# Five unsplit weight pairs, a reciprocal on ScalarE, the attention state kept in the keys' rows, port waits both ways, and a new instruction order, in a fused attention and MLP kernel

## The chip, the cores and the metric

The kernel runs on one core of one Trainium2 chip. The metric is the time of one execution on the device in microseconds (us). Engines are named as the profile names them: PE (TensorE, the matmuls), PEld (its weight loads), DVE (VectorE), ACT (ScalarE), POOL (GpSimd), SP (SyncE, which here only issues DMAs). Each engine carries out its own instruction list in order, and waits on semaphores for the others.

## The reference

Two stages. The first is a gated linear attention with a recurrence over 768 steps; the second is an MLP with a rational activation on the result.

```python
# q, k, v, alpha: (4, 8, 768, 48)
for t in range(S):
    state = alpha[:, :, t, :, None] * state + np.einsum('bhd,bhe->bhde', k[:, :, t], v[:, :, t])
    y[:, :, t] = np.einsum('bhd,bhde->bhe', q[:, :, t], state)
x = y.transpose(0, 2, 1, 3).reshape(3072, 384)
h = x @ w_in                       # w_in (384, 2048)
P = a[0] + a[1] * h + a[2] * h**2 + a[3] * h**3
Q = 1.0 + abs(b[0]) * abs(h) + abs(b[1]) * h**2
out = (P / (Q + 1e-06)) @ w_out    # w_out (2048, 384)
```

## The kernel before

**Attention.** The 3072 tokens are handled in 24 chunks of 128 tokens (g = 0 to 23, six for each batch entry). For a chunk, DVE forms running products of alpha with two scans (`suf`, line 470, and `pre`, line 482), which POOL or DVE multiply into k and q (`k`, line 491, and `q`, line 494). PE transposes k (`kt`), forms scores within each half chunk (`s`), the k-v products of both halves (`vk`) and at last the output (`am`, line 594). The state between chunks goes through three steps: `d` (line 564, POOL) multiplies the old state `st_s` by the chunk's total decay and writes it into the rows of the tile `sv` that `am` reads for the first half; `km` (line 605, DVE) adds the first half's k-v product and writes the rows for the second half; `kv` (line 609, DVE) adds the second half's product and writes `st_s`. The heads stand in two row groups (j = 0 and 1), so each of the three steps is two instructions of 48 rows by 192 columns, and a small copy `tot` (line 553 on ACT, 555 on DVE) brings the totals of one row group into the other's rows first. After `am`, ACT and DVE bring the result from PSUM into the MLP's input as a rounded part and a remainder (`xh`, `xl`).

**MLP.** It consists of 96 units, u = 0 to 95; each yields 128x512 activations. In a "wide" unit (128 features by 512 tokens) products are formed in three passes on operands of type fp32r: both operands are split into a rounded part and a remainder, and input and output take nine matmuls of 512 columns each (`in`, line 703; `oh` and `ol`, line 722, and lines 716 and 731 for the last 512 tokens). A "plain" unit (256 features by 256 tokens) uses unsplit words: six matmuls of 256 columns on the way in (line 676), six on the way out (line 689), each with two PE records in the trace. `JP = 4` pairs of feature blocks are worked plain for the first two token groups, which makes units 0 to 7 plain; unit 8 is the first wide one. Between `in` and `oh` a unit goes through ACT: `ah` (line 758), `t1` (761), `q1` (767, or POOL, 765); POOL: `qm` (770, the denominator); DVE: `t2` (781), `t3` (785); ACT: `ars` (788, one over the root), `sq` (791, its square, so an approximate reciprocal); DVE: `p` (795), `t` (798) and `g` (804), which correct the reciprocal and finish the quotient. Wide units need two steps more, the rounded part `gh` (807, ACT) and the remainder `gl` (811, POOL or DVE). The products `in` of unit u use a PSUM bank that `g` of unit u - 3 sets free.

**Weights.** Each pair of feature blocks has an input block (i0 to i7) and an output block (o0 to o7). They arrive as 64-bit words; ACT (`abs`, line 278), DVE (`low` 286, `sign` 292, or ACT 290, and `join` 306) make 32-bit words of them, and ACT and POOL split these (`hi` 321, `lo` 326). A plain pair's words are kept, and brought back later by a DMA to be split for the wide units.

**Order.** All of it is about 2,800 steps. A table of numbers (`ORDER`) gives the order in which `Plan.run` writes them out, and a bit for each says on which of two engines it runs. Some DVE steps are marked `lock` (the joins and shifts of the weights, the splits, and k, q and remainders where DVE does them): `Plan.run` makes the next POOL step in the table wait for such a step, and names as the reason a port that DVE and POOL share. A guard on alpha's range (`gu`, line 857, 36 ACT instructions), whose sum becomes the word `ok` (line 873), decides at the end whether a slow general path must run; it does not run here.

## Time and profile before

| | |
|---|---|
| median of 3 runs | 529.93 us (528.15 to 530.42) |
| profiled execution, whole | 529.12 us |
| its span, first to last instruction | 527.2 us |
| PE busy | 501.1 us, 95% |
| DVE busy | 492.3 us, 93% |
| ACT busy | 440.8 us, 84% |
| POOL busy | 424.8 us, 81% |
| mean granted PE clock | 0.993 |

Busy times are unions over the span. PE's matmuls overlap in their pipeline and their ends are modelled, so a stretch in which PE is busy throughout says that work follows work, not that it runs at its peak; the time from one matmul to the next is read from the chain, where matmuls in a row are merged into one piece with their count. The profiled execution took 1.92 us more than its span.

### The profile page before, as it was taken

The page shows a single profiled execution, that of the slowest core. Times are in us where ns is not written, and L with a number is a line of the kernel's source. Part 1 is how long each engine was busy: PE and PEld are TensorE (multiplying, and loading weights), DVE is VectorE, ACT ScalarE, POOL GpSimd, SP SyncE. Part 2 cuts the span into 40 slices and gives each one's busy share as a digit, 9 for nine tenths or more (in the row PEclk, how much of TensorE's full clock was granted, in tenths as well). Part 3 has the DMA queues.
Part 4 walks back from the last instruction along what each step waited for, and adds up shares of the span by engine and source line. Part 5 has one row for each costly group of instructions (what it writes and reads, how often), then busy time and mean ns, then how long its engine had stood idle before and what let it go on. Part 6 is the DMA issues. An engine that isn't in the chain of part 4 may idle for free.

```text
span 527.2 us, 13661 instructions
## 1 busy us (share of the span) xinstructions
PE 501.1 (95%) x5082; PEld 410.9 (78%) x5082; DVE 492.3 (93%) x773; ACT 440.8 (84%) x805; POOL 424.8 (81%) x421
## 2 busy tenths in 40 slices
PE   7877988988999999999999999999999999999996
PEld 7865876766878778787878778878888778888996
DVE  4999899999999999999999899999999999898885
ACT  4998999998999878887888798897888887987782
POOL 3556667899999998889879789888888887876782
PEclk9997999999999999999999999999999999999999
DMA  9989684565554444454446345351545201023001
GB/s 266 278 228 291 141 201 87 120 170 119 117 146 112 106 84 96 94 100 116 98 92 117 95 97 101 85 118 30 110 97 116 47 6 39 0 62 60 2 2 63
DMA packets 145656, 56.81 MB, mean 108 GB/s; under 512 B 133424, under 2 KB 138160, under 8 KB 145584
## 3 DMA queue, kind: packets, MB, share of 16 engines
q1 hardware_dynamic: 145440, 55.78, 45.1%
q8 instruction: 41, 0.67, 0.6%
...
HBM read 47.98 MB, written 4.72 MB: 100 GB/s over the span
## 4 chain that ended last, share of the span: by engine, by line
PE 76%; DVE 8%; DMA 5%; ACT 4%; SPq 3%; issue 2%; POOL 1%; DVEq 0%; POOLq 0%
PE ps L703 31%; PE ps L722 26%; PE ps L716 6%; PE ps L594 3%; DMA wi_words<-in_moe_w_in_dram 2%; PE ps L512 2%; SPq L409 2%; PE ps L689 2%; PE ps L576 2%; PE ps L545 1%; DMA raw_a<-in_alpha_dram 1%; ACT wo_words L290 1%; DVE t L804 1%; DMA wo_words<-in_moe_w_out_dram 1%; DVE ps L798 1%
## 5 line engine op out<-in xcount | busy, mean ns | idle before, releaser
L703 PE MATMUL ps<-x,wi 128*128 128x512 f32 x792 | 203.6, 397 | 2.8 <-DVE t L804 2.7
L703 PEld LDWEIGHTS ps<-x,wi 128*128 128x128 f32 x792 | 145.9, 188 | 36.2 <-DVE t L804 4.6
L722 PE MATMUL ps<-gh_gl,wo 128*128 128x512 f32 x648 | 170.1, 399 | 0.2 <-ACT gh_gl L807 0.2
L722 PEld LDWEIGHTS ps<-gh_gl,wo 128*128 128x128 f32 x648 | 119.2, 188 | 27.0 <-ACT gh_gl L807 0.3
L770 POOL TENSOR_TENSOR qm<-qm,ah 128x512 f32<-128x512 f32 x96 | 124.3, 1296 | 13.6 <-ACT qm L767 4.4
L811 POOL TENSOR_TENSOR gh_gl<-t,gh_gl 128x512 fp32r<-128x512 f32 x83 | 109.0, 1313 | 15.4 <-ACT gh_gl L807 12.7
L758 ACT ACTIVATE ah<-ps 128x512 f32<-128x512 f32 x96 | 57.2, 596 | 26.4 <-PE ps L703 25.8
L795 DVE SCALAR_TENSOR_TENSOR t<-t,coef,ps 128x512 f32<-128x512 f32 x96 | 70.6, 736 | 5.7 <-ACT ps L791 4.5
L761 ACT ACTIVATE t<-ps,coef 128x512 f32<-128x512 f32 x96 | 65.9, 687 | 8.5 <-PE ps L703 4.3
L785 DVE SCALAR_TENSOR_TENSOR t<-t,coef,ps 128x512 f32<-128x512 f32 x96 | 70.8, 739 | 1.0
L765 POOL TENSOR_SCALAR qm<-ah,bab 128x512 f32<-128x512 f32 x61 | 48.3, 793 | 29.0 <-ACT ah L758 15.8
L781 DVE TENSOR_TENSOR t<-t,ps 128x512 f32<-128x512 f32 x96 | 64.9, 676 | 4.6 <-ACT t L761 2.8
L788 ACT ACTIVATE ps<-qm 128x512 f32<-128x512 f32 x96 | 57.9, 604 | 12.6 <-DVE t L785 5.6
L804 DVE SCALAR_TENSOR_TENSOR t<-ps,t 128x512 f32<-128x512 f32 x96 | 65.5, 683 | 1.1
L798 DVE SCALAR_TENSOR_TENSOR ps<-qm,ps 128x512 f32<-128x512 f32 x96 | 65.8, 686 | 0.2
L807 ACT ACTIVATE gh_gl<-t 128x512 fp32r<-128x512 f32 x88 | 55.2, 628 | 5.8 <-DVE t L804 5.5
L791 ACT ACTIVATE ps<-ps 128x512 f32<-128x512 f32 x96 | 56.2, 586 | 2.0
L539 POOL TENSOR_SCALAR_AFFINE_SELECT tqk<-tqk 64x512 f32<-64x512 f32 x48 | 33.2, 692 | 12.7 <-ACT tqk L533 7.1
L470 DVE TENSOR_TENSOR_SCAN tg<-ta,ps 128x528 f32<-128x528 f32 x24 | 29.7, 1242 | 6.7 <-ACT ta L452 6.7
L494 POOL TENSOR_TENSOR tqk<-tqk,fp 128x512 f32<-128x512 f32 x22 | 29.1, 1322 | 7.2 <-DVE wi_words L306 6.1
L491 POOL TENSOR_TENSOR tqk<-tqk,tg 128x512 f32<-128x512 f32 x23 | 29.8, 1294 | 5.9 <-ACT tqk L452 5.5
L594 PEld LDWEIGHTS ps<-tqk,sv 128*32 128x32 f32 x1536 | 23.4, 112 | 13.8 <-issue 5.0
(112 smaller groups left out, 724.4 us busy)
## 6 DMA issues: line engine op xcount, KB each, us to landing
...
```

What stands on the lines that cost most here:

```text
L703: nc.tensor.matmul(h_of(u), w(key)[:, kt * FU + f % FU, :], x[:, kt, xp, :], start=(n == 0), stop=(n == len(todo) - 1),)
L722: nc.tensor.matmul(bank(O_BANKS[dt]), w(("o", f // FU))[:, f % FU, dt * P : (dt + 1) * P], g, start=(f == 0 and first_w), stop=(f == NF - ...
L758: nc.scalar.activation(buf(s, "ah", u), h_of(u), AF.Abs)
L761: nc.scalar.activation(buf(s, "t1", u), h_of(u), AF.Identity, bias=a2, scale=a3_reg)
L770: nc.gpsimd.tensor_tensor(buf(s, "qm", u), buf(s, "qm", u), buf(s, "ah", u), op=ALU.mult)
L781: nc.vector.tensor_tensor(t, t, h_of(u), op=ALU.mult)
L785: nc.vector.scalar_tensor_tensor(t, t, a1, h_of(u), op0=ALU.add, op1=ALU.mult)
L788: nc.scalar.activation(h_of(u), buf(s, "qm", u), AF.Abs_reciprocal_sqrt, bias=1.0 + 1e-6)
L795: nc.vector.scalar_tensor_tensor(t, t, a0, h_of(u), op0=ALU.add, op1=ALU.mult)
L798: nc.vector.scalar_tensor_tensor(h_of(u), buf(s, "qm", u), 1.0 + 1e-6, h_of(u), op0=ALU.add, op1=ALU.mult)
L804: nc.vector.scalar_tensor_tensor(t, h_of(u), 2.0, t, op0=ALU.subtract, op1=ALU.mult, reverse0=True)
L811: eng.tensor_tensor(buf(s, "gl", u).rearrange("p a b -> p (a b)"), buf(s, "t1", u), gh, op=ALU.subtract)
```

## The change

Five edits and a new table.

1. `JP = 5`: pairs 0 to 4 are plain for the first two token groups. Units 0 to 9 are plain, 10 to 95 wide.
2. `rcp` replaces `ars` and `sq`: one ACT instruction of the function Reciprocal. The coefficients are scaled by 2^-24 at the start, so that numerator and denominator stand at that scale.
3. The state stays in the rows in which the keys' products come (112 rows, both row groups and the gap between them): `d`, `km` and `kv` are one instruction each, of 112 rows by 192 columns, on three tiles `st`. New steps `dc` and `mc` (`place`) copy it into the rows of `sv`, two instructions of 48 rows by 192 columns each, on ACT or POOL: 50 instructions on ACT and 38 on POOL in the new table. `tot` and its tiles are gone.
4. `Plan.run` adds waits both ways: a locked step on DVE also waits for the last POOL step ahead of it in the table.
5. `one_eps`, `prime` and the waits are adapted to these.
6. `ORDER` is another table.

The diff, of the table only one line:

```diff
--- before.py
+++ after.py
@@ -51,3 +51,3 @@
         info = mybir.DependencyInfo(mybir.DependencyClass.Sync, mybir.DependencyReason.DATA)
-        held = None
+        held = last = None
         for n in order:
@@ -64,6 +64,11 @@
             if mode["lock"]:
+                if last is not None:
+                    tc.add_manual_dep(new[0], last.name, info, reason="shared port")
+                    last = None
                 held = new[-1]
-            elif mode["eng"] == "POOL" and held is not None:
-                tc.add_manual_dep(new[0], held.name, info, reason="shared port")
-                held = None
+            elif mode["eng"] == "POOL":
+                if held is not None:
+                    tc.add_manual_dep(new[0], held.name, info, reason="shared port")
+                    held = None
+                last = new[-1]
             done.add(key)
@@ -72,66 +77,64 @@
 ORDER = [
-    'c-jTQ1E3u`3;@t3X_~gPZQHhO+qS*k?fK2NZQHhO+xFi-XN*!Rx^gOtLN!)RQeLr&t;VUzDykZ<jGCubs3|I%TBxR~`D&t',
...
+    'c-jq?gO(*a5CGGi?sSs1ZQHhO+qS)XcV>35wr$(CZQHi--Zxa8Qx!=~R!X6YsiG-Sq*yr>Lm3rCMOS0hI5l3)SBunQ6;-WN',
...
 ]
@@ -166,3 +169,3 @@
 T2P = range(0)
-JP = 4
+JP = 5
 HALF = 3
@@ -232,4 +235,8 @@
 
+    SMALL = 2.0 ** -24
+    Q_ONE = (1.0 + 1e-6) * SMALL
+
     def abs_coef():
-        nc.scalar.activation(bab, coef[:, 4:6], AF.Abs)
+        nc.scalar.activation(coef[:, 0:4], coef[:, 0:4], AF.Copy, scale=SMALL)
+        nc.scalar.activation(bab, coef[:, 4:6], AF.Abs, scale=SMALL)
         load_reg(a3_reg, coef[0:1, 3:4])
@@ -357,5 +364,4 @@
     sv = ring("sv", NV, [P, 2, H, DP])
-    st_s = work.tile([P, H, D], F32, name="st_s")
-    tots = ring("tots", 2, [P, NC4])
     KW = P - GAP
+    st_0, st_m, st_e = ring("st", 3, [P, NC4, D])
     kts = ring("kt", NSC, [P, NC4 * KW + GAP])
@@ -549,17 +555,17 @@
 
-    def totals(eng, g):
-        o, x = tots[g % 2][rows_of(1)], totals_of(g)[rows_of(0)]
-        if eng is nc.scalar:
-            eng.activation(o, x, AF.Copy)
-        else:
-            eng.tensor_copy(o, x)
-
     def decay(eng, g):
-        o, r = state_of(g, 0), rows_of(1)
-        if first(g):
-            eng.memset(o, 0.0)
+        t = totals_of(g)[0:KW].unsqueeze(2).to_broadcast([KW, NC4, D])
+        eng.tensor_tensor(st_0[0:KW], st_e[0:KW], t, op=ALU.mult)
+
+    def place(eng, g, c):
+        o = state_of(g, c)
+        if c == 0 and first(g):
+            nc.gpsimd.memset(o, 0.0)
             return
         for j in range(2):
-            t = totals_of(g) if j else tots[g % 2]
-            eng.tensor_tensor(o[:, j::2], st_s[r, j::2], t[r].unsqueeze(2).to_broadcast([D, NC4, D]), op=ALU.mult)
+            x = (st_m if c else st_0)[rows_of(j)]
+            if eng is nc.scalar:
+                eng.activation(o[:, j::2], x, AF.Copy)
+            else:
+                eng.tensor_copy(o[:, j::2], x)
 
@@ -567,4 +573,4 @@
 
-    def kv_of(c, j):
-        return bank(SCB + c)[rows_of(j), KV0 : KV0 + NC4 * D].rearrange("p (a d) -> p a d", d=D)
+    def kv_of(c):
+        return bank(SCB + c)[0:KW, KV0 : KV0 + NC4 * D].rearrange("p (a d) -> p a d", d=D)
 
@@ -600,11 +606,9 @@
     def kv_mid(g):
-        for j in range(2):
-            if first(g):
-                nc.vector.tensor_copy(state_of(g, 1)[:, j::2], kv_of(0, j))
-            else:
-                nc.vector.tensor_tensor(state_of(g, 1)[:, j::2], state_of(g, 0)[:, j::2], kv_of(0, j), op=ALU.add)
+        if first(g):
+            nc.vector.tensor_copy(st_m[0:KW], kv_of(0))
+        else:
+            nc.vector.tensor_tensor(st_m[0:KW], st_0[0:KW], kv_of(0), op=ALU.add)
 
     def kv_add(g):
-        for j in range(2):
-            nc.vector.tensor_tensor(st_s[rows_of(1), j::2], state_of(g, 1)[:, j::2], kv_of(1, j), op=ALU.add)
+        nc.vector.tensor_tensor(st_e[0:KW], st_m[0:KW], kv_of(1), op=ALU.add)
 
@@ -786,7 +790,11 @@
 
-    def act_ars(u, s):
-        nc.scalar.activation(h_of(u), buf(s, "qm", u), AF.Abs_reciprocal_sqrt, bias=1.0 + 1e-6)
-
-    def act_sq(u, s):
-        nc.scalar.activation(h_of(u), h_of(u), AF.Square)
+    def inverse_of(o, x, bias):
+        imm = [mybir.ImmediateValue(dtype=F32, value=v) for v in (bias, 1.0, 0.0)]
+        nc.scalar.add_instruction(mybir.InstActivation(
+            name=nc.get_next_instruction_name(), engine=nc.scalar.engine, func=AF.Reciprocal,
+            ins=[nc.scalar.lower_ap(x), *imm], outs=[nc.scalar.lower_ap(o)],
+        ))
+
+    def act_rcp(u, s):
+        inverse_of(h_of(u), buf(s, "qm", u), Q_ONE)
 
@@ -798,3 +806,3 @@
         nc.vector.scalar_tensor_tensor(
-            h_of(u), buf(s, "qm", u), 1.0 + 1e-6, h_of(u), op0=ALU.add, op1=ALU.mult
+            h_of(u), buf(s, "qm", u), Q_ONE, h_of(u), op0=ALU.add, op1=ALU.mult
         )
@@ -949,3 +957,3 @@
                     act_q1(nc.scalar, u, s)
-                    for step in (pool_qm, dve_t2, dve_t3, act_ars, act_sq):
+                    for step in (pool_qm, dve_t2, dve_t3, act_rcp):
                         step(u, s)
@@ -975,4 +983,4 @@
     add("floor_s", "POOL", 0.1, nc.gpsimd.memset, (floor_s, FLOOR))
-    add("one_eps", "POOL", 0.1, nc.gpsimd.memset, (one_eps, 1.0 + 1e-6))
-    add("prime", "ACT", 1.5, nc.scalar.activation, (first_act, one_eps, AF.Abs_reciprocal_sqrt), ["one_eps"])
+    add("one_eps", "POOL", 0.1, nc.gpsimd.memset, (one_eps, 1.0))
+    add("prime", "ACT", 1.5, inverse_of, (first_act, one_eps, 0.0), ["one_eps"])
     add(("lim", 0), "POOL", 0.1, nc.gpsimd.memset, (lim[:, 0:1], LOW * STEEP))
@@ -1044,3 +1052,3 @@
             add("fl", "DVE", 0.17, set_floor, (), ["floor_s"] + [("cp", *x, p, cc) for x in nat_users[SCB + 1] for p in (None, 0, 1) for cc in range(2)], lock=True)
-        add(("suf", g), "DVE", 1.25, suffix, (g,), ready["a"] + ["consts"] + ["fl"] * (g >= G3) + [("k", g - NTG), ("d", g - NTG), ("tot", g - NTG), ("inv", g - NTG)])
+        add(("suf", g), "DVE", 1.25, suffix, (g,), ready["a"] + ["consts"] + ["fl"] * (g >= G3) + [("k", g - NTG), ("d", g - NTG), ("inv", g - NTG)])
         add(("inv", g), "DVE", 0.18, inverse, (g,), [("suf", g)])
@@ -1062,10 +1070,15 @@
             add(("sm", g, c), "POOL", 0.66, sc_mask, (g, c), [("se", g, c)])
+        here = [("am", g - NV), ("set", "v", g % NV)]
+        if not first(g):
+            add(("d", g), "POOL", 0.5, decay, (g,), [("suf", g), ("kv", g - 1), ("km", g - 1), ("dc", g - 1)], alt=("DVE", 0.3, True))
         if g:
-            if not first(g):
-                add(("tot", g), "ACT", 0.18, totals, (g,), [("suf", g), ("d", g - 2)], alt=("DVE", 0.16, False))
-            add(("d", g), "POOL", 1.1, decay, (g,), [("suf", g), ("tot", g), ("kv", g - 1), ("km", g - 1), ("am", g - NV), ("set", "v", g % NV)], alt=("DVE", 0.72, True))
-        add(("km", g), "DVE", 0.71, kv_mid, (g,), [("vk", g), ("d", g), ("am", g - NV), ("set", "v", g % NV)])
+            if first(g):
+                add(("dc", g), "POOL", 0.3, place, (nc.gpsimd, g, 0), here)
+            else:
+                add(("dc", g), "ACT", 0.6, place, (g, 0), [("d", g)] + here, alt=("POOL", 0.95, False))
+        add(("km", g), "DVE", 0.4, kv_mid, (g,), [("vk", g), ("d", g), ("kv", g - 1), ("mc", g - 1)])
+        add(("mc", g), "ACT", 0.6, place, (g, 1), [("km", g)] + here, alt=("POOL", 0.95, False))
         if not last(g):
-            add(("kv", g), "DVE", 0.71, kv_add, (g,), [("vk", g), ("km", g), ("d", g)])
-        add(("am", g), "PE", SV[1], attn_mm, (g,), [("sm", g, 0), ("sm", g, 1), ("s", g), ("qc", g), ("d", g), ("km", g), ("sv", g, 0), ("sv", g, 1), ("xl", g - 1), ("xh", g - 1)], lat=0.13)
+            add(("kv", g), "DVE", 0.4, kv_add, (g,), [("vk", g), ("km", g), ("d", g)])
+        add(("am", g), "PE", SV[1], attn_mm, (g,), [("sm", g, 0), ("sm", g, 1), ("s", g), ("qc", g), ("dc", g), ("mc", g), ("sv", g, 0), ("sv", g, 1), ("xl", g - 1), ("xh", g - 1)], lat=0.13)
     for g in range(NGC):
@@ -1108,3 +1121,3 @@
         add(("ah", u), "ACT", 0.6, act_ah, (u, fb), ins + [("qm", u - AB)])
-        add(("t1", u), "ACT", 0.78, act_t1, (u, fb), ins + [("gl", u - TB), ("gh", u - TB), "coef"] + ([("oh", u - TB, 1)] if TB <= u < TB + NUP else []))
+        add(("t1", u), "ACT", 0.78, act_t1, (u, fb), ins + [("gl", u - TB), ("gh", u - TB), "bab"] + ([("oh", u - TB, 1)] if TB <= u < TB + NUP else []))
         add(("q1", u), "ACT", 0.82, act_q1, (u, fb), [("ah", u), ("t", u - QB), "bab"], alt=("POOL", 0.8, False))
@@ -1117,5 +1130,4 @@
         add(("t3", u), "DVE", 0.74, dve_t3, (u, fb), [("t2", u)])
-        add(("ars", u), "ACT", 0.7, act_ars, (u, fb), [("qm", u), ("t3", u), "one_eps"])
-        add(("sq", u), "ACT", 0.6, act_sq, (u, fb), [("ars", u)])
-        add(("p", u), "DVE", 0.74, dve_p, (u, fb), [("sq", u)])
+        add(("rcp", u), "ACT", 0.7, act_rcp, (u, fb), [("qm", u), ("t3", u), "bab"])
+        add(("p", u), "DVE", 0.74, dve_p, (u, fb), [("rcp", u)])
         add(("t", u), "DVE", 0.69, dve_t, (u, fb), [("p", u)])
```

How the table moves instructions is shown at three places; `[waits ...]` names the engines or DMA queues on whose semaphores a row waits.

DVE in the first part of the program, before, from the step `p` of unit 0 on (`t_100` to `t_102` are the buffers of units 0 to 2, `wr`, `parts` and the words belong to weight blocks):

```order
L795 SCALAR_TENSOR_TENSOR t_100<-t_100,coef,ps 128x512 [waits Activation_49]
L605 TENSOR_TENSOR sv_91<-sv_91,ps 48x4x48 [waits Pool_49] x2
L798 SCALAR_TENSOR_TENSOR ps<-qm_103,ps 128x512
L470 SCALAR_TENSOR_TENSOR tg_86<-ta_83,ps 128x528 [waits DVE_49]
L804 SCALAR_TENSOR_TENSOR t_100<-ps,t_100 128x512 [waits DVE_49]
L306 SCALAR_TENSOR_TENSOR wr_77<-wr_77,wi_words 128x768 [waits Activation_49]
L286 TENSOR_SCALAR wo_words<-wo_words 128x768 [waits DMAHW7_49]
L609 TENSOR_TENSOR st_s<-sv_91,ps 48x4x48 x2
L795 SCALAR_TENSOR_TENSOR t_101<-t_101,coef,ps 128x512 [waits Activation_49]
L781 TENSOR_TENSOR t_102<-t_102,ps 128x512 [waits PE_49]
L798 SCALAR_TENSOR_TENSOR ps<-qm_104,ps 128x512 [waits Pool_49]
L785 SCALAR_TENSOR_TENSOR t_102<-t_102,coef,ps 128x512 [waits DVE_49]
```

DVE at the same place, after:

```order
L803 SCALAR_TENSOR_TENSOR t_100<-t_100,coef,ps 128x512 [waits Activation_49]
L293 TENSOR_SCALAR wi_words<-wi_words 128x768 [waits DMAHW5_49,Pool_49]
L806 SCALAR_TENSOR_TENSOR ps<-qm_103,ps 128x512
L610 TENSOR_TENSOR st_94<-st_93,ps 112x192 [waits PE_49]
L476 SCALAR_TENSOR_TENSOR tg_86<-ta_83,ps 128x528 [waits DVE_49,PE_49]
L812 SCALAR_TENSOR_TENSOR t_100<-ps,t_100 128x512 [waits DVE_49]
L613 TENSOR_TENSOR st_95<-st_94,ps 112x192 [waits DVE_49]
L313 SCALAR_TENSOR_TENSOR wo_words<-wr_78,wo_words 128x2x384 [waits Activation_49,Pool_49]
L293 TENSOR_SCALAR wo_words<-wo_words 128x768 [waits DMAHW6_49]
L293 TENSOR_SCALAR wo_words<-wo_words 128x768 [waits DMAHW3_49]
L803 SCALAR_TENSOR_TENSOR t_101<-t_101,coef,ps 128x512 [waits Activation_49]
L485 RECIPROCAL ta_83<-tg_86 128x4 [waits DVE_49]
```

The two L605 rows and the two L609 rows of a chunk became one each (L610 and L613), score copies (L541) came to DVE, several joins and shifts stand in a row, and the first of such a run waits for POOL.

ACT at the end of the program, before; L749 copies the last tile's output, L755 stores a half of it, L807 is `gh`:

```order
L788 ACTIVATE ps<-qm_104 128x512 [waits DVE_49,Pool_49]
L791 ACTIVATE ps<-ps 128x512 [waits Activation_49]
L807 ACTIVATE gh_gl<-t_101 128x512 [waits DVE_49,PE_49]
L807 ACTIVATE gh_gl<-t_102 128x512 [waits DVE_49,PE_49]
L749 ACTIVATE parts<-ps 128x384 [waits DMAHW3_49,DMAHW4_49,DMAHW2_49,DMAHW5_49,DMAHW1_49,DMAHW7_49,DMAHW0_49,PE_49]
L749 ACTIVATE parts<-ps 128x192 [waits DMAHW6_49,DMAHW1_49,DMAHW7_49,DMAHW0_49,DVE_49]
L755 DMA out_dram<-parts 128x192 [waits Activation_49]
```

ACT at the end, after; L865 is the guard `gu`, L753 and L759 the copy and the store of the last tile, L815 `gh`:

```order
L793 ACTIVATE ps<-qm_104 128x512 [waits DVE_49,Pool_49]
L865 ACTIVATE wr_78,beyond<-wr_78,lim 128x512 [waits DMAHW2_49]
L815 ACTIVATE gh_gl<-t_101 128x512 [waits DVE_49,PE_49]
L865 ACTIVATE wr_77,beyond<-wr_77,lim 128x512 [waits DMAHW3_49]
L815 ACTIVATE gh_gl<-t_102 128x512 [waits DVE_49,PE_49]
L753 ACTIVATE parts<-ps 128x384 [waits DMAHW5_49,DMAHW4_49,DMAHW6_49,DMAHW1_49,DMAHW7_49,DMAHW0_49,PE_49]
L753 ACTIVATE parts<-ps 128x192 [waits PE_49]
L865 ACTIVATE wr_77,beyond<-wr_77,lim 128x512 [waits Activation_49]
L865 ACTIVATE wr_78,beyond<-wr_78,lim 128x512
L759 DMA out_dram<-parts 128x192 [waits Activation_49]
```

Four guard instructions stand among the last, two of them between the last copy and its store. The last copy waited for DVE and now waits for PE.

SP at the start, before:

```order
L416 DMA raw_a_80<-in_alpha_dram 128x8x96
L416 DMA raw_qk_81<-in_k_dram 128x8x96
L416 DMA raw_qk_81<-in_q_dram 128x8x96
L416 DMA raw_second<-in_alpha_dram 128x8x96
L266 DMA wi_words<-in_moe_w_in_dram 128x3x512 x2
L456 DMA sv_91<-in_v_dram 64x8x48 x2
L416 DMA raw_second<-in_k_dram 128x8x96
L416 DMA raw_second<-in_q_dram 128x8x96
```

SP at the start, after:

```order
L422 DMA raw_qk_81<-in_k_dram 128x8x96
L422 DMA raw_a_80<-in_alpha_dram 128x8x96
L422 DMA raw_qk_81<-in_q_dram 128x8x96
L462 DMA sv_91<-in_v_dram 64x8x48
L273 DMA wi_words<-in_moe_w_in_dram 128x3x512
L462 DMA sv_91<-in_v_dram 64x8x48
L422 DMA raw_second<-in_alpha_dram 128x8x96
L273 DMA wi_words<-in_moe_w_in_dram 128x3x512
```

The load of k now goes out ahead of that of alpha, and the first weight block ahead of the second alpha load.

## Rows read from the trace of the kernel before

**Rows 1.** Six windows: start:end, length, PE, PEld, DVE, ACT, POOL busy us, clock, DMA.
```profile
0.00:13.20 13.20, 10.14 (x94) 9.70 (x97) 5.54 (x8) 6.07 (x11) 4.55 (x23) 1.00 0.93 266
13.20:52.70 39.50, 30.40 (x560) 26.83 (x552) 37.85 (x60) 36.33 (x61) 22.74 (x26) 0.91 0.94 266
52.70:105.40 52.70, 48.73 (x528) 39.47 (x526) 50.80 (x82) 51.17 (x76) 38.88 (x36) 1.00 0.61 137
105.40:136.60 31.20, 26.90 (x348) 20.40 (x347) 30.60 (x48) 28.43 (x50) 30.29 (x26) 1.00 0.54 135
136.60:512.00 375.40, 374.49 (x3511) 304.49 (x3511) 358.79 (x566) 313.38 (x603) 323.22 (x308) 1.00 0.38 81
512.00:527.20 15.20, 10.47 (x61) 10.02 (x59) 8.69 (x15) 5.45 (x10) 5.11 (x5) 0.99 0.16 56
```

**Rows 2.** Chain that ended last, three of its pieces: start us, us, what.
```profile
97.83 2.59 PE ps L689 x12
...
188.07 2.04 PE ps L703 x9
...
205.48 2.09 PE ps L722 x9
```

**Rows 3.** Groups of DVE instructions by line and shape: busy us, mean ns, idle.
```profile
L462 DVE STREAM_TRANSPOSE ta<-raw_a 128x512 f32<-128x512 f32 x20 | 14.1, 705 | 1.8 <-DMA raw_qk<-in_q_dram 1.8
...
L605 DVE TENSOR_TENSOR sv<-sv,ps 48x192 f32<-48x192 f32 x40 | 14.1, 352 | 2.5 <-ACT ps L791 1.4
...
L609 DVE TENSOR_TENSOR st_s<-sv,ps 48x192 f32<-48x192 f32 x40 | 14.1, 353 | 1.0
...
L811 DVE TENSOR_TENSOR gh_gl<-t,gh_gl 128x512 fp32r<-128x512 f32 x5 | 3.7, 744 | 0.8 <-ACT gh_gl L807 0.8
...
L494 DVE TENSOR_TENSOR tqk<-tqk,fp 128x512 f32<-128x512 f32 x2 | 1.4, 688 | 0.1
```

**Rows 4.** The same view, ACT.
```profile
L788 ACT ACTIVATE ps<-qm 128x512 f32<-128x512 f32 x96 | 57.9, 604 | 12.6 <-DVE t L785 5.6 <-POOL qm L770 5.0 <-POOL tqk L491 0.6
...
L791 ACT ACTIVATE ps<-ps 128x512 f32<-128x512 f32 x96 | 56.2, 586 | 2.0
...
L857 ACT ACTIVATE wr<-wr,lim 128x512 bf16<-128x512 f32 x36 | 25.8, 717 | 0.4 <-DMA wr<-in_alpha_dram 0.3
...
L522 ACT ACTIVATE tqk<-tqk 64x256 f32<-64x256 f32 x48 | 20.0, 417 | 2.9 <-PE ps L512 1.9
...
L553 ACT ACTIVATE tots<-tg 48x4 f32<-48x4 f32 x18 | 3.7, 205 | 0.4
```

**Rows 5.** The same view, three shapes of the DVE join in line 306.
```profile
L306 DVE SCALAR_TENSOR_TENSOR parts<-parts,wo_words 128x768 uint32<-128x768 uint32 x2 | 3.5, 1736 | 0.0
...
L306 DVE SCALAR_TENSOR_TENSOR wo_words<-wr,wo_words 128x768 uint32<-128x768 uint32 x2 | 2.7, 1348 | 0.0
...
L306 DVE SCALAR_TENSOR_TENSOR wi_words<-wr,wi_words 128x768 uint32<-128x768 uint32 x2 | 1.9, 942 | 0.0
```

**Rows 6.** Timeline near 120 us, DVE and POOL: start us, us, engine, line.
```profile
120.59 2.47 DVE L306 SCALAR_TENSOR_TENSOR parts<-parts,wo_words 128x768 uint32<-128x768 uint32 x1
...
120.42 1.83 POOL L326 TENSOR_TENSOR wi<-wr,wi 128x768 fp32r<-128x768 f32 x1
```

**Rows 7.** Timeline of the first 8 us, two pieces.
```profile
1.43 0.57 SPq L416 DMA_DIRECT2D raw_qk<-in_k_dram  x1
...
7.94 2.40 DVE L470 TENSOR_TENSOR_SCAN tg<-ta,ps 128x528 f32<-128x528 f32 x2 [6.37 <-ACT ta L452]
```

**Rows 8.** Timeline of the end, four pieces.
```profile
521.16 1.59 DVE L751 COPY parts<-ps 128x384 f32<-128x384 f32 x3 [0.89 <-PE ps L731]
...
522.67 0.14 DVE L873 TENSOR_SCALAR ok<-ps 1x1 int32<-1x1 f32 x1
...
522.78 0.33 ACT L749 ACTIVATE parts<-ps 128x192 f32<-128x192 f32 x1 [0.60 <-DVE ok L873]
...
523.15 0.39 ACTq L755 DMA_DIRECT2D out_dram<-parts  x1
```

More of the change, by code (lines that the diff above doesn't have):

```diff
@@ L133 @@
[L133 to L136 removed]
+    'c-jq?gO(*a5CGGi?sSs1ZQHhO+qS)XcV>35wr$(CZQHi--Zxa8Qx!=~R!X6YsiG-Sq*yr>Lm3rCMOS0hI5l3)SBunQ6;-WN',
+    'vD6y1L`_i3l~+?#WHnVSP)pS+bzMzT6IC}{sFnq~V-HNN(yBCSePFFh7g(WsVlV8CeXws(KkSbKaRg3NGt_D|00-e&eNL}a',
@@ L137 @@
+    '<L-nz>8`o!?xB0)p1No5z5C!kx!vxRyWzm2f9_7Zo9?4~;l8?W?xlO>wErCO#eH|TBG~_MKOK4T*8g(GpK-7MhwA-p7t_b`',
+    'cU)}$+r=Fj&);=_+#8q5zjdkoJNMVc@$r2EpU_A0k$oDUZe${#)@Se;eR`kCNAXd8VxPq4_IZ3>|Id|h$|v>7d>LQX=lA)1',
+    'W}n4p^>uwTAKl0B1$`l3-k0;)d?jDN7xooKR`x}FQD4zl@%4NIpWQd~jeId*)fe|od{f`pH}lDT3ZK%K@Hu==pUao@rF=EN',
+    '(y#K>eGOmJFZ0WNX<y4X_bq%&-^#c4wS67m#<%q~T|3|2ckms3C*Rq3@m+m4-`)4{J$)a)!mswdd~d(juk-7Dec#vr2X6hG',
+    'js',
 ]
```

118 lines of the change are left out of this document (55 added, 63 removed).

## The prediction

> **What bounds the kernel now.** I read the busy times by stage first, since PE (501 us) and DVE (492 us) are both close to the span of 527.2 us and the question is which of them is waited for, and where. In [rows 1] PE is idle for 3.06 us of the first 13.2 us, 9.10 us up to 52.7, 3.97 up to 105.4 and 4.30 up to 136.6: 20.4 us together. From 136.6 to 512 us it is idle for 0.9 us of 375.4. So from about 136 us on PE has one matmul behind another, and nothing that another engine gains there can shorten the run. Before that, DVE is the engine without rest: 5.54 us busy of the first 13.2, where it waits for the first alpha ([rows 7]), and then 37.85 of 39.5, 50.80 of 52.7 and 30.60 of 31.2, that is 4.15 us idle in 123.4 us. ACT is close to it (51.17 of 52.7 in the third window), POOL only in the fourth (30.29 of 31.2). So the early part is paced by DVE, the long rest by PE.
>
> The point where one hands over to the other is about unit 17: its input matmuls wait for `g` of unit 14, the last DVE step of that unit (units three apart share a PSUM bank); its end is where I put the border at 136.6 us. Behind unit 17's input PE has the same work in both orders: units 18 to 95, the outputs from unit 13's last group on, chunks 8 to 23. The forecast is therefore how much earlier DVE finishes unit 14, plus what happens at both ends of the program.
>
> **PE's own work.** Two wide units become plain, 24 matmuls of 256 columns with two records each. Twelve records in a row took 2.59 us, 0.216 each, so 48 x 0.216 = 10.4 us. Out go 36 wide matmuls: nine input ones took 2.04 us, nine output ones 2.09 us, so 2 x (2.04 + 2.09) = 8.3 us [rows 2]. PE has 2.1 us more to do. Both units lie ahead of the handover, where PE is idle for 20.4 us, so I cost them at nothing; if DVE no longer covers them, they cost 2.1 us.
>
> **DVE up to unit 14's last step.** Counted in the two orders up to the fifteenth L804 (L812 after): `km` of eight chunks and `kv` of seven are 30 instructions of 0.352 to 0.353 us, 10.6 us [rows 3]. After, it is `km` of eight and `kv` of six, single instructions of the same 192 columns on 112 rows. No row has that shape; L494, at 128 rows and 512 columns, took 0.688, so 320 more columns cost 0.336 whatever the rows are, and I take 0.353: 14 x 0.353 = 4.9 us. At worst, at a 512-column price, they would be 9.6. Two remainders on DVE go (2 x 0.744 = 1.5), and one transpose of alpha falls behind the point (0.7). Added are three score copies, one k and two q products on DVE, six instructions of 512 columns at 0.688, 4.1 us. Sum: -5.7 - 1.5 - 0.7 + 4.1 = -3.8 us; with the worst price, +0.9.
>
> **The port waits.** Two shapes of the join took 1736 and 1348 ns where a third took 942, two of each, so 2 x 0.79 + 2 x 0.41 = 2.4 us were lost [rows 5]. [Rows 6] show one case: the join began at 120.59 while POOL ran a split from 120.42 to 122.25, and it lasted 2.47 us, 1.5 over the ordinary. In the part up to unit 14, the table before has 20 places at which a locked DVE step follows a POOL step in the order; the new one has 12 (the shifts and joins stand together, as the order shows). If loss goes with such places, 2.4 x 8/20 = 1.0 us is saved; bounds are a loss as below and a gain of 2.4. The Trainium skill, "SBUF — State Buffer", section "SBUF: two separate sides", calls the shared port an exclusive lock: whoever starts first has it for the whole instruction, and the other blocks. The join in [rows 6], which ends about 0.8 us after POOL's split, agrees. By that rule a wait for a POOL instruction that is already running costs what the block cost, and only regrouping saves; what the rule does not excuse is a wait for a POOL step that has not begun. Taken strictly, it would put this term at 0 and the time at 527.0.
>
> **ACT.** `sq` goes: 96 x 0.586 = 56.2 us. `rcp` is put at the 0.604 us of `ars` (L788); no row has the function Reciprocal, and between the 0.586 of L791 and double, 1.2, ACT would at worst give the 56 us back. The 50 copies of `place` lie between 205 ns (4 columns) and 417 ns (256 columns), about 0.37 for 192, 18.5 us [rows 4]. ACT is relieved by over 30 us in all, but DVE idles only 4.15 us in the stage that counts, so I credit nothing; at most those 4.15 us come back. POOL gives 40 state products for 20 of the same columns and 38 copies, and hands 19 `q1` steps to ACT, so it is not worse off where it is full. The copies stand between `km` and `am`: if a chunk's copy came late, PE would wait up to 2 x 0.37 us; the cover is the units' matmuls that the table has between `vk` and `am`.
>
> **The two ends.** At the start the load of k is issued ahead of alpha's; its issue takes 0.57 us [rows 7], and DVE's first scan waits for alpha through PE and ACT: +0.5 us, between 0 and 1. At the end, the last copy on ACT (522.78) no longer waits for DVE and can start some 0.5 us earlier, but two guard instructions of 0.72 us [rows 4] now stand between it and its store, which was issued at 523.15 [rows 8]: +0.9. The word `ok` (522.67 before) now follows those guards and comes, with a sum, a matmul and a comparison behind them, some 2 us later, of which 0.9 was hidden by the last store's issue (523.15 and 0.39), so about +1.1. I take +1.1 us. The other two guards stand ahead of the last `gh` steps; PE has twelve output groups there to hide them.
>
> **Sum.** -3.8 - 1.0 + 0.5 + 1.1 = -3.2 us against the profiled execution's 529.12 us: 525.9. The median of the runs shown, 529.93, lies 0.8 above that execution and the lowest 1.0 below, so no shift is due; I say 526.0.
>
> **Rivals.**
> - *DVE's gain is real but PE takes it.* If the idle PE time does not lie where units 8 and 9 are, the 2.1 us come back: 528.1, no change. For it: 12.2 of the 20.4 us are before 52.7, ahead of those units. Against it: 8.3 us are idle from there to 136.6, so PE has room for 2.1 more.
> - *DVE waits for POOL.* The 12 new waits up to unit 14 (place: a shift or join at the head of its run, with all of DVE's list behind it, and then `p` to `g` of the current units, for which PE waits). If the POOL step that is named is late by a whole instruction, about 1.3 us (the 1.83 of [rows 6] is the longest kind), this costs up to 12 x 1.3 = 15.6 us. It decides from 0.35 us a wait (4.2 us, the saved 3.2 and the lost credit of 1.0); at 0.7 us, 8.4 us, the time is 529.1 - 2.2 + 8.4 = 535. For it: POOL is full from 105 to 136 us, so it runs behind. Against it: from 13 to 105 us POOL is busy for 61.6 of 92.2 us, and most of the waits are there.
> - *ACT was the hidden brake.* DVE's 4.15 idle us and the whole 2.4 us of blocking go: 526.0 - 4.15 - 1.4 = 520.5. For it: ACT at 97% in the third window, and a chain that is one ACT step shorter. Against it: an in-order DVE list never idles to nothing.
>
> **Chances and range.** The forecast's case, 522 to 527.3, has 0.50; PE taking the gain 0.27; the POOL waits 0.12; ACT as the brake 0.11. About 0.5% (2.65 us) is what a measurement of this kernel can tell from no change, so faster means below 527.3. That gives faster 0.61, same 0.28, slower 0.11. The likeliest case's own range is 522 to 527.3; the stated one reaches from 520.5 to 530.5, which leaves out most of the waits' case and the extreme of the brake.
>
> **What would show it.** Right: PE without idle time from about 132 us on, `g` of unit 14 about 4 us earlier; the sum of DVE's busy time near 477 us (44 instructions fewer at 0.353); the joins near 0.95 us; the last store about 1 us later behind PE's last matmul than before. Wrong: idle time on DVE ahead of L293 or L313 that ends on POOL, above 0.35 us each; PE waiting for `place` (L568 or L570) or idle after 140 us; ACT's L793 above 0.7 us; or a handover that is not earlier at all.

## The result, and the profile after

The changed kernel took 524.33 us (median of 4, 523.89 to 525.09) against 530.16 (median of 4, the three runs shown above and one more, 528.15 to 530.42) of the kernel before on the same chip: ratio 0.9905, 95% interval 0.988 to 0.9931, so 5.0 us faster (3.7 to 6.4). Its profiled execution took 523.89 us with a span of 521.9; before, 529.12 and 527.2.

The windows of [rows 1], now of the changed kernel: start:end, length, then busy us of PE, PEld, DVE, ACT and POOL, granted clock, DMA.

```profile
0.00:13.20 13.20, 10.24 (x72) 9.63 (x72) 4.96 (x8) 5.10 (x9) 4.67 (x26) 1.00 0.91 250
13.20:52.70 39.50, 31.07 (x572) 27.49 (x576) 35.91 (x58) 32.91 (x57) 15.22 (x19) 0.91 0.96 269
52.70:105.40 52.70, 50.22 (x555) 41.12 (x547) 51.20 (x80) 51.45 (x78) 39.83 (x42) 1.00 0.62 158
105.40:136.60 31.20, 31.20 (x376) 25.25 (x377) 30.63 (x48) 28.74 (x53) 28.60 (x25) 1.00 0.53 125
136.60:512.00 375.40, 375.24 (x3518) 305.04 (x3517) 349.09 (x536) 289.90 (x557) 315.40 (x308) 1.00 0.38 81
512.00:521.90 9.90, 4.37 (x26) 3.94 (x25) 1.81 (x5) 2.81 (x7) 1.64 (x2) 0.96 0.24 84
```

PE was not busy for 20.4 us of the first 136.6; now it is 2.96 + 8.43 + 2.48 + 0 = 13.9, and from 105 us on there is no gap. PE's own busy time rose from 501.1 to 502.3 us. 6.5 us less without work and 1.2 more work are the 5.3 us of the span.

The same along the prediction's border, each from the times of single instructions: unit 14's `g` (the fifteenth instruction of line 812) ended at 130.2 us, 6.3 earlier than before (136.5). From there to PE's last output matmul it took 386.0 us, before 385.8. From that matmul to the end of the span it took 5.7 us, before 4.9. So, unrounded, -6.34 + 0.16 + 0.88 = -5.30: everything gained was gained ahead of the border.

The border itself has moved. From 75 to 130 us, all of it ahead of unit 14's last step, PE is now idle for 0.3 us, where it was idle for 6.5 (columns as above, first the changed kernel, then the kernel before):

```profile
75.00:130.00 55.00, 54.70 (x643) 44.47 (x643) 53.20 (x82) 52.48 (x86) 45.98 (x40) 1.00 0.55 132
```

```profile
75.00:130.00 55.00, 48.52 (x582) 37.38 (x584) 54.10 (x84) 51.87 (x87) 47.17 (x41) 1.00 0.52 121
```

PE works without a gap from about 75 us on, not from about 130.

Groups of DVE, ACT and POOL instructions by line and shape (busy us, mean ns, idle before them), to be held against [rows 3 to 5]:

```profile
L793 ACT ACTIVATE ps<-qm 128x512 f32<-128x512 f32 x96 | 57.7, 602 | 35.3 <-DVE t L789 17.0 <-POOL qm L774 15.1 <-POOL tqk L500 2.1
...
L568 ACT ACTIVATE sv<-st 48x192 f32<-48x192 f32 x50 | 18.0, 360 | 2.5 <-POOL st L558 0.8 <-DVE st L608 0.7 <-DVE st L610 0.3
...
L570 POOL COPY sv<-st 48x192 f32<-48x192 f32 x38 | 13.0, 342 | 2.1 <-DVE st L610 0.2
...
L613 DVE TENSOR_TENSOR st<-st,ps 112x192 f32<-112x192 f32 x20 | 6.9, 344 | 0.3
L610 DVE TENSOR_TENSOR st<-st,ps 112x192 f32<-112x192 f32 x20 | 6.8, 340 | 0.9 <-ACT ps L793 0.7 <-PE ps L518 0.2
...
L313 DVE SCALAR_TENSOR_TENSOR wo_words<-wr,wo_words 128x768 uint32<-128x768 uint32 x3 | 2.9, 958 | 0.5 <-ACT wo_words L297 0.3 <-POOL qm L774 0.2
...
L313 DVE SCALAR_TENSOR_TENSOR parts<-parts,wo_words 128x768 uint32<-128x768 uint32 x2 | 1.9, 955 | 0.1
```

A state step of 112 rows takes 0.34 us, where one of 48 rows took 0.35, and there are half as many. All 16 joins take 0.94 to 0.96 us; before, two of them took 1.74 and 2.47. The reciprocal costs 602 ns, what the root cost.

The end of the program, timeline (start us, us, what), to be held against [rows 8]:

```profile
516.21 0.33 ACT L753 ACTIVATE parts<-ps 128x192 f32<-128x192 f32 x1 [0.56 <-PE ps L735]
516.44 0.71 ACT L865 ACTIVATE wr<-wr,lim 128x512 bf16<-128x512 f32 x1
516.57 0.38 ACTq L759 DMA_DIRECT2D out_dram<-parts  x1
...
517.14 0.71 ACT L865 ACTIVATE wr<-wr,lim 128x512 bf16<-128x512 f32 x1
...
517.98 0.19 DVE L875 TENSOR_REDUCE tot_beyond<-beyond 128x1 f32<-128x36 f32 x1 [1.04 <-ACT wr L865]
...
518.45 0.15 DVE L881 TENSOR_SCALAR ok<-ps 1x1 int32<-1x1 f32 x1 [0.28 <-PE ps L878]
```

The last store (516.57) goes out right behind the last copy on ACT (516.21 and 0.33), while the first of two guard instructions is already running. But `ok` comes at 518.45, 2.3 us behind the end of the last output matmul (516.18); before it came 0.3 us behind it.

### The profile page after: what moved, and what is told of

The parts are those of the page before. It is cut to its first block, busy times and chain, and to the rows that moved or that the text cites. A ratio compares the mean times of both kernels' runs of the same rounds, so it can differ in the third digit from the quotient of the medians.

```text
span 521.9 us, 13513 instructions
## 1 busy us (share of the span) xinstructions
PE 502.3 (96%) x5094; PEld 412.5 (79%) x5094; DVE 473.6 (91%) x729; ACT 410.9 (79%) x756; POOL 405.4 (78%) x419
## 4 chain that ended last, share of the span: by engine, by line
PE 73%; DMA 9%; DVE 6%; ACT 4%; SPq 4%; POOL 2%; issue 2%; DVEq 0%; ACTq 0%; POOLq 0%
PE ps L707 30%; PE ps L726 28%; DMA wi_words<-in_moe_w_in_dram 5%; PE ps L600 4%; PE ps L720 2%; PE ps L518 2%; PE ps L693 2%; PE ps L582 2%; DMA raw_a<-in_alpha_dram 2%; SPq L415 2%; DVE t L789 1%; DMA sv<-in_v_dram 1%; PE ps L551 1%; DVE t L785 1%; DMA wo_words<-in_moe_w_out_dram 1%
## 5 line engine op out<-in xcount | busy, mean ns | idle before, releaser
L707 PE MATMUL ps<-x,wi 128*128 128x512 f32 x774 | 199.2, 397 | 0.1
L707 PEld LDWEIGHTS ps<-x,wi 128*128 128x128 f32 x774 | 142.9, 188 | 33.0 <-DVE t L812 1.4
L726 PE MATMUL ps<-gh_gl,wo 128*128 128x512 f32 x630 | 164.9, 399 | 0.0
L726 PEld LDWEIGHTS ps<-gh_gl,wo 128*128 128x128 f32 x630 | 116.0, 188 | 27.3 <-POOL gh_gl L819 0.7
L765 ACT ACTIVATE t<-ps,coef 128x512 f32<-128x512 f32 x96 | 65.4, 684 | 14.7 <-POOL gh_gl L819 6.9
L815 ACT ACTIVATE gh_gl<-t 128x512 fp32r<-128x512 f32 x86 | 53.7, 626 | 6.3 <-DVE t L812 5.9
L769 POOL TENSOR_SCALAR qm<-ah,bab 128x512 f32<-128x512 f32 x42 | 32.3, 770 | 19.6 <-ACT ah L762 7.8
L545 POOL TENSOR_SCALAR_AFFINE_SELECT tqk<-tqk 64x512 f32<-64x512 f32 x48 | 31.5, 656 | 19.0 <-ACT tqk L539 8.5
L771 ACT ACTIVATE qm<-ah,bab 128x512 f32<-128x512 f32 x54 | 39.0, 722 | 0.5
L720 PE MATMUL ps<-wo,gh_gl 128*128 128x384 f32 x180 | 33.8, 337 | 0.0
L720 PEld LDWEIGHTS ps<-wo,gh_gl 128*128 128x128 f32 x180 | 31.9, 188 | 1.2
```

The lines of the kernel that those rows point to most:

```text
L707: nc.tensor.matmul(h_of(u), w(key)[:, kt * FU + f % FU, :], x[:, kt, xp, :], start=(n == 0), stop=(n == len(todo) - 1),)
L720: nc.tensor.matmul(bank(T_BANKS[tt], DM), g[:, tt * P : (tt + 1) * P], w(("o", f // FU))[:, f % FU, :], start=(f == 0 and first_w), stop=( ...
L726: nc.tensor.matmul(bank(O_BANKS[dt]), w(("o", f // FU))[:, f % FU, dt * P : (dt + 1) * P], g, start=(f == 0 and first_w), stop=(f == NF - ...
L765: nc.scalar.activation(buf(s, "t1", u), h_of(u), AF.Identity, bias=a2, scale=a3_reg)
```

## The experiments

Twelve kernels ran, in three groups, each beside the kernel before on the same chip. Where runs of different groups are compared, their ratios to the kernel before are, with 530 us for a ratio of 1. "Later" and "earlier" of a unit's `g` are against the changed kernel's trace unless said otherwise.

**The port waits.** The changed kernel without the wait of DVE for POOL (in `Plan.run` three lines are gone):

```diff
             if mode["lock"]:
-                if last is not None:
-                    tc.add_manual_dep(new[0], last.name, info, reason="shared port")
-                    last = None
                 held = new[-1]
```

> The changed kernel without the wait of a locked DVE step for the POOL step ahead of it (POOL's wait for DVE stays, the table too). If a wait for a POOL instruction that runs costs what the block on the port costs, and only the grouping in the new table saved: within 1 us of the changed kernel's 524.3. If the waits themselves gave the 2.4 us that the joins lost before: about 2 us slower, 526.5, with joins above 1 us in the trace. If the waits cost time (POOL steps that run late): faster, 523 or less.

524.4 us, ratio 0.9898 (0.987 to 0.9927): no difference. Its longest join took 1.07 us, and the 16 together 15.4 us, against 15.3 with the wait and 17.7 before. So it is the new order that keeps POOL's long steps out of the joins' way, and not the wait.

The kernel before, in its order, with the same lines added:

> The kernel before, its own table, with the waits both ways. If the lock costs the same as the wait: within 1 us of 530.2. If the waits alone take the joins' loss away: about 2 us faster, 528. If its 20 places, not arranged for the waits, make DVE wait for late POOL steps at 0.35 us or more each: 3 to 8 us slower than before.

548.8 us, ratio 1.0363 (1.0333 to 1.0393), 19 us slower, more than twice the most that was expected. Its waits of DVE for POOL (us in total, times, longest):

```profile
DVE gh_gl L816 <- POOL qm L770: 7.0, 3, 4.7
...
DVE parts L311 <- POOL tqk L544: 5.3, 1, 5.3
...
DVE wo_words L311 <- POOL tqk L544: 4.0, 1, 4.0
...
DVE tqk L496 <- POOL tqk L544: 1.9, 1, 1.9
```

The joins take 0.96 us here too, and 2.4 us of blocking are gone; for them DVE waits over 18 us, 5.3 in one piece, for POOL steps that stand ahead of it in the order and come late. The prediction's rival on POOL describes this kernel. What the Trainium skill says of the port ("SBUF — State Buffer", section "SBUF: two separate sides": who starts first holds it, the other blocks for the length of that instruction) fits the 1.74 and 2.47 us of before and their absence here. The trace of the kernel before shows it for more than these two: five of its 16 joins start while POOL has an instruction running, and each ends 0.80 to 0.82 us after that instruction's end, however long it still ran. Two of them, beside the one in [rows 6]:

```profile
36.66 1.29 POOL L491 TENSOR_TENSOR tqk<-tqk,tg 128x512 f32<-128x512 f32 x1
...
37.02 1.74 DVE L306 SCALAR_TENSOR_TENSOR wo_words<-wr,wo_words 128x768 uint32<-128x768 uint32 x1
...
73.53 0.79 POOL L765 TENSOR_SCALAR qm<-ah,bab 128x512 f32<-128x512 f32 x1
...
74.12 1.00 DVE L306 SCALAR_TENSOR_TENSOR parts<-parts,wo_words 128x768 uint32<-128x768 uint32 x1
```

So the order that parts the two saves 2.4 us of DVE's time, and waits that part them in an order not made for it cost eight times that.

**The code edits in the order of before.** The joined state alone: `d`, `km` and `kv` as in the change, `tot` gone, `dc` and `mc` put right behind `km`.

```diff
-        for j in range(2):
-            nc.vector.tensor_tensor(st_s[rows_of(1), j::2], state_of(g, 1)[:, j::2], kv_of(1, j), op=ALU.add)
+        nc.vector.tensor_tensor(st_e[0:KW], st_m[0:KW], kv_of(1), op=ALU.add)
```

> The order of before with one edit of the change alone: the state is kept in the keys' rows (one DVE instruction for km and for kv instead of two), its copies into the attention tile stand right behind km on ACT or POOL, the copy of the totals is gone. Theory (DVE paces the run up to about 136 us, and the halved state steps are the main term): DVE does 30 fewer half-width instructions up to unit 14's last step, 5.7 us less, PE's work is unchanged, so 525 to 527 us against 530. Rival (the gain comes from the new order, not from this edit): within 1 us of 530, since the copies sit in ACT's list and the attention matmuls wait for them.

542.8 us, ratio 1.0247 (1.0218 to 1.0275). Both expectations fell. Three windows of it, columns as above:

```profile
13.20:52.70 39.50, 30.88 (x548) 26.43 (x541) 34.77 (x52) 37.37 (x64) 23.57 (x27) 0.96 0.91 260
52.70:105.40 52.70, 47.25 (x513) 38.28 (x512) 46.41 (x69) 49.65 (x74) 37.41 (x37) 0.97 0.59 134
105.40:136.60 31.20, 25.59 (x275) 18.92 (x273) 27.41 (x42) 26.94 (x48) 25.84 (x23) 0.89 0.54 136
```

DVE's busy time fell as it should: 34.77 + 46.41 + 27.41 = 108.6 us against 119.3 before. But PE did not get its work earlier; it was busy for 103.7 us against 106.0 and ran at half its clock for 13.7 us instead of 6.8 (granted clock 0.96, 0.97 and 0.89). Unit 14's `g` came 6.4 us later than before, and another 7.3 us were lost behind it. What DVE waited for, over the whole run, are two ACT steps of each unit, the square (L787; L791 before) and `t1` (L757; L761 before), here and in the kernel before (us in total, times, longest):

```profile
DVE t L791 <- ACT ps L787: 19.4, 27, 2.0
DVE t L777 <- ACT t L757: 16.5, 20, 2.9
```

```profile
DVE t L795 <- ACT ps L791: 4.5, 7, 1.4
DVE t L781 <- ACT t L761: 2.8, 6, 1.2
```

So DVE has less to do here and waits more than it saves, most of it for ACT, which has copies of the state to make as well.

The reciprocal alone (`rcp` where `ars` stood, `sq` gone):

```diff
-    def act_sq(u, s):
-        nc.scalar.activation(h_of(u), h_of(u), AF.Square)
+    def act_rcp(u, s):
+        inverse_of(h_of(u), buf(s, "qm", u), Q_ONE)
```

> The order of before with the reciprocal alone: the square behind the root is gone, 96 ACT instructions of 0.586 us less, 17 of them before the handover (10 us of ACT time there). Theory (ACT was not the brake): within 1 us of 530. Rival (ACT was the hidden brake): below 527, with DVE's idle time before 136 us down by 2 us or more.

529.7 us, ratio 0.9987 (0.9967 to 1.0008): no difference clear of noise, with 56 us less work on ACT. Nor did DVE's idle time between 13.2 and 136.6 us fall (5.5 us, before 4.2). ACT was not the brake of the kernel before.

Both edits:

> The order of before with both code edits: state kept in the keys' rows (as in the run that had it alone, 542.8 us) and the reciprocal. Theory 1 (the copies of the state cost time because ACT's list was full; the reciprocal gives it 10 us before the handover): most of the 12.6 us go, 528 to 532. Theory 2 (the order of the lists does it: the copies and what waits for them stand at places that were not arranged for them): still above 536. The changed kernel, with the same edits in its own order, takes 524.3.

536.2 us, ratio 1.0126 (1.0101 to 1.0152), between the two theories. The reciprocal that is worth nothing alone is worth 6.4 us (1.0247 - 1.0126, at 530) once ACT has the state's copies to make. DVE's wait for ACT's last step ahead of `p`, 19.4 us above, is 4.1 here, that for `t1` is still there:

```profile
DVE t L779 <- ACT t L759: 22.9, 27, 2.9
...
DVE t L797 <- ACT ps L787: 4.1, 6, 1.0
```

6.7 us over the kernel before remain as the price of both edits in the old order, with the copies where this run put them. The 11.7 us from there to the changed kernel belong to what was not in this run: the new order, the fifth pair and the waits. The waits are worth nothing by the first run; order and fifth pair were not run apart.

**The state steps put back into the changed kernel**, in its order (`tot` and the wide `d` where `d` stood, `km` and `kv` in two instructions, no copies):

```diff
-        nc.vector.tensor_tensor(st_e[0:KW], st_m[0:KW], kv_of(1), op=ALU.add)
+        for j in range(2):
+            nc.vector.tensor_tensor(st_s[rows_of(1), j::2], state_of(g, 1)[:, j::2], kv_of(1, j), op=ALU.add)
```

> The changed kernel and its order with the state steps of before put back (two DVE instructions each for km and kv, the decay and the copy of the totals as before, no copies into the attention tile). Theory: DVE has 5.7 us more up to unit 14's last step, so unit 14's quotient comes 5 to 6 us later than in the changed kernel and the time is 529 to 530.5 us against 524.3. Rival (the order carries the gain): under 526.5.

544.6 us, ratio 1.0276 (1.0251 to 1.0301). The first half held: unit 14's `g` came 5.7 us later. The second did not, and the rival's figure is further off still; by unit 80 the lag had grown to 21 us. In that stretch PE, which the prediction had without a gap, waits (us in total, times, longest; the two largest):

```profile
PE ps L708 <- DVE t L813: 4.3, 11, 1.0
PE ps L599 <- POOL tqk L544: 2.3, 2, 2.0
```

Line 813 is `g`. DVE's state steps are 10.9 us longer behind the border, and the lag grows by 15.4 there, so the room that the new order leaves DVE is too small for them, and POOL's and ACT's attention steps come late as well. How the 15.4 us divide between these was not run apart.

**DVE's own time.** `km` of eight chunks three times over, 16 instructions of 0.34 us, once in chunks 0 to 7 and once in 12 to 19:

```diff
+        for _ in range(EXTRA if g < 8 else 1):
+            nc.vector.tensor_tensor(st_m[0:KW], st_0[0:KW], kv_of(0), op=ALU.add)
```

> The changed kernel with the state step km of chunks 0 to 7 written three times instead of once: 16 more DVE instructions of 0.34 us or a little more with their own waits, 5.5 to 6.5 us, all ahead of unit 14's last step. Handover theory (DVE sets the pace up to there, PE after it): 5 to 6.5 us slower, 529.5 to 531. If PE or the loads set the early pace: under 2 us slower. If DVE's total counts: 5.5 us, as in the late one.

528.75 us, ratio 0.998 (0.9965 to 0.9994): 4.0 us by the ratio, 4.4 by the medians, less than the handover theory's 5 to 6.5. The extra instructions came to 5.7 us in the trace. Unit 14's `g` is 4.6 us later, 0.5 of it already at the first scan, and the lag stays at 4.5 to the end. DVE's time ahead of the border is worth 0.7 to 0.8 us for each us.

> The same 16 extra DVE instructions in chunks 12 to 19, which lie between about 200 and 430 us. Handover theory: DVE has some 26 us idle there while PE has none, so within 1 us of 524.3. If DVE's total counts: 5.5 us slower.

526.43 us, ratio 0.9949 (0.993 to 0.9968): 2.1 to 2.3 us, more than either expected. 1.0 us of the profiled execution's lag is there at the start; 1.9 us grow between units 28 and 64. DVE's time behind the border is cheaper, but not free. PE's waits there (us, times, longest; line 815 is `g`) are less than half of the 1.9; the rest is not accounted for:

```profile
PE ps L602 <- POOL tqk L545: 0.4, 1, 0.4
PE ps L710 <- DVE t L815: 0.4, 1, 0.4
```

**PE's own time.** Eight more matmuls in the inputs of units 8 and 9 (the first product three times, result unchanged), and sixteen in units 40 to 55:

```diff
-        for kt in range(KT):
+        for kt in ([0] * 2 if u in (8, 9) else []) + list(range(KT)):
...
-        for n, (kt, w, xp) in enumerate(todo):
+        for n, (kt, w, xp) in ([(-1, todo[0])] if 40 <= u < 56 else []) + list(enumerate(todo)):
```

> The changed kernel with eight more input matmuls of 256 columns in units 8 and 9 (the first product of each group three times instead of once, result unchanged), 8 x 0.432 = 3.5 us of PE work between 80 and 92 us. The prediction's step (DVE paces this part and PE's extra work is hidden): under +1 us, 524.3 to 525.3. Rival (PE takes it; for it the changed kernel's trace shows PE idle for only 0.2 us between 75 and 130 us): +2.5 to +3.5, 526.8 to 527.8.

526.99 us, ratio 0.9959 (0.9941 to 0.9976): 2.7 us by the medians, 2.9 by the ratio, the rival's figure. `g` of unit 10 is 2.5 us later and all that follows too. The window in question:

```profile
52.70:105.40 52.70, 51.11 (x571) 42.89 (x571) 48.92 (x74) 49.02 (x74) 38.52 (x41) 1.00 0.63 157
```

PE is busy for 0.9 us more of it than in the changed kernel, DVE for 2.3 us less: DVE waits, by the releasers, for ACT steps (L539, L765) that read PE's products, and so in the end for PE.

> The changed kernel with sixteen more input matmuls of 512 columns in units 40 to 55 (the first product of each unit twice, result unchanged), 16 x 0.227 = 3.6 us of PE work between about 250 and 340 us. Theory (PE has one matmul behind another there and sets the time): +3.3 to +3.9, 527.6 to 528.2. Rival (matmuls that seem to follow each other have slack in them, or DVE is as tight): under +2 or over +5.

528.31 us, ratio 0.999 (0.9971 to 1.0009), 4.0 us by the medians, 4.5 by the ratio, a little over the theory's range. 0.8 us of the profiled execution's lag is there at the start; 3.5 us grow between units 40 and 56, of the 3.6 put in. From the border on PE sets the time nearly to the full.

**The ends.** Two runs of the changed kernel with the last four guards and their sum at other places, and alpha's first load ahead of k's. First the guards among units 87 to 90:

> The changed kernel with seven steps at other places: alpha's first load is issued ahead of k's, and the last four guard instructions with the sum behind them stand among units 86 to 92 instead of at the end. Theory (the verdict word now ends the run, 2.25 us behind the last matmul, and the start lost one issue of 0.57): the end gains 1.0 to 1.4 us, the start 0.5, so 522.4 to 523 us against 524.3. Rival 1 (the last store ends the run, not the verdict): only the start's 0.5, 523.8. Rival 2 (the guards delay PE in the dense part, 3 us of ACT work there): the gain is lost, 524 or more.

524.36 us, ratio 0.9894 (0.9871 to 0.9917): nothing by the medians, 0.6 us by the ratio, inside the noise of both; the second rival's figure. The end did shrink, from 5.7 to 4.7 us behind PE's last matmul, but between units 84 and 92 the lag of `g` grew by 0.9 us, and PE waited (us, times, longest):

```profile
PE ps L706 <- DVE t L811: 0.6, 1, 0.6
```

And the start was no earlier. The first matmuls on PE, of the changed kernel and of this one (start us, us; line 432, here 431, is the warm-up on the identity, line 439, here 438, the transposes of alpha):

```profile
1.78 4.28 PE L432 MATMUL ps<-ident 128*128 128x128 f32 x20 [1.78 <-POOL ident masks.py:199]
5.96 1.97 PE L439 MATMUL ps<-ident,raw_a 128*128 128x128 f32 x16
```

```profile
1.78 4.53 PE L431 MATMUL ps<-ident 128*128 128x128 f32 x20 [1.78 <-POOL ident masks.py:199]
6.10 2.29 PE L438 MATMUL ps<-ident,raw_a 128*128 128x128 f32 x16
```

Alpha landed at 4.6 us here instead of 5.9, but its transposes stand behind 20 warm-up matmuls that take until about 6. The warm-up starts as soon as POOL has built the identity (1.78; before, 1.51). In the changed kernel alpha's landing and the end of the warm-up fall together, so either alone would hold the transposes. So in the second run alpha's load stays ahead, the identity is built first, and each guard stands ahead of an ACT step that waited 1.5 us or more (places in the decoded table, not lines of code; the guards' loads and their sum move too):

```diff
+gu.17.0
 rcp.87
...
+gu.17.1
 rcp.88
...
+gu.16.0
 gh.88
...
+gu.16.1
 rcp.91
```

> The changed kernel with its last four guard instructions (0.9 us each on ACT) in front of steps for which ACT waited 1.5 us or more (the reciprocals of units 87, 88 and 91, and the rounding of unit 88), their sum behind DVE's last quotient, where DVE waits 2.8 us, alpha's first load ahead of k's, and the identity built first, so that the warm-up matmuls start 0.27 us earlier. Theory: the end gains 1.0 us as in the run with the guards among units 86 to 92, and this time PE does not wait for it: 523 to 523.6 against 524.3. Rival (any ACT work there makes PE wait): 524 or more, with PE idle again between 470 and 505 us.

522.71 us (median of 6), ratio 0.9882 (0.9852 to 0.9913), span 520.6. The profiled gain of 1.3 us, a little more than expected, is where it was expected: 0.3 at the start (all `g` 0.3 earlier) and 1.0 at the end, with no wait of PE above 0.1 us from 87 us to its last output matmul. The end, with `ok` 0.3 us behind the last copy:

```profile
515.95 0.33 ACT L752 ACTIVATE parts<-ps 128x192 f32<-128x192 f32 x1 [0.55 <-PE ps L734]
516.31 0.38 ACTq L758 DMA_DIRECT2D out_dram<-parts  x1
...
516.59 0.14 DVE L880 TENSOR_SCALAR ok<-ps 1x1 int32<-1x1 f32 x1
```

It is the fastest kernel here by its median, and clearly faster than the kernel before; against the changed kernel (1.6 us by the medians, 1.2 by the ratio) the intervals overlap, so there it rests on the trace.

## Why the prediction came out right

Forecast 526.0, measured 524.3. The place of the gain and the sign were right; the forecast for unit 14's `g` was 4.3 us earlier, and it was 6.3. That the time came within 1.7 us is in part luck: one term came out three times as large as forecast, and two that were put at nothing were not nothing. Term by term, for DVE in sums of the durations of its instructions up to that `g`:

- **The handover and what follows it.** Right: 385.8 and 386.0 us from there to PE's last matmul, and the late PE run. But "nothing that another engine gains there" does not mean that nothing it loses there counts: two runs showed that it does.
- **PE's 2.1 us at nothing.** This step failed. In the changed kernel PE has 0.3 us of idle time between 75 and 130 us, and 3.5 us more work there cost 2.5 to 2.9. If the same share holds (not shown: nothing was taken away there), the two plain units cost 1.5 to 1.7 us, which the larger gain of DVE covered. The rival "PE takes it" had the mechanism, and too small a gain against it.
- **DVE's instruction count.** -5.7 for the state was 10.59 to 4.84, -5.75; the remainders -1.65 for -1.5; alpha's transpose -0.75 for -0.7; the copies and products +3.6 for +4.1, since a `tot` on DVE (0.52) went too. Sum -4.6 for -3.8. Of scans and unit steps both orders have the same number up to there; small groups add 0.1.
- **The port.** The mis-sized term: -1.0 forecast (its upper bound was 2.4), -3.0 measured, 2.4 of it in the joins and 0.6 in the shifts. Crediting by the share of places was wrong, since nearly all of the loss lay in two joins of sixteen and both went. The added waits did nothing (first run), so that only regrouping saves held; to put the term at 0 and the time at 527.0 for it was wrong, since the new table does regroup.
- **ACT.** Credited nothing, and alone the reciprocal is worth nothing. But it was no spare part: in the old order the state's copies find no room without it (6.4 us). And DVE, which was to idle no more than before, waits for it longer in the changed kernel: 3.1 us for the reciprocal between 13 and 137 us, where 1.4 us were spent on the like before.

```profile
DVE t L803 <- ACT ps L793: 3.1, 4, 1.7
```

  The prediction weighed the edits one by one and did not see that one pays for the other.
- **The start.** +0.5 forecast; the first scan came 0.7 later, 8.65 for 7.94 [rows 7]. The reason given, k's load ahead of alpha's, is not the whole of it: alpha landed 1.4 us later (5.9 for 4.5), but with alpha first alone nothing was gained. The warm-up behind the later identity, and the clock (below), held the transposes as long.
- **The end.** +1.1 forecast, 0.9 measured, by the half of the reasoning that spoke of `ok`. The other half, that the guards delay the last store, was wrong.
- **DVE waiting for POOL.** Nothing in the new order (first run), 19 us in the old one (second run). By the waits of the second run (4.7 us and 5.3 for single POOL steps) what decides is whether the POOL step that is named comes in time, which the prediction could not read from the number of places.

Together the durations fell by 4.6 + 3.0 - 0.1 = 7.5 us. DVE's records overlap a little, by 1.0 us more after than before, so the time in which DVE was busy from the first scan to unit 14's `g` fell by 8.4 us, from 124.2 to 115.8. Its idle time there rose by 1.4, from 4.4 to 5.7, and the first scan came 0.7 later: -8.4 + 1.4 + 0.7 = -6.3 us up to the border.

What stays open: how the 11.7 us between "both edits in the old order" and the changed kernel divide between order and fifth pair. In the old order the copies were put at one place only; a better place was not tried. And of the lag behind the border in the two DVE runs only a part is seen as waits of PE.
